# A decode layer's tile framework replaced by a hand-written dependency tracker

## The chip, the cores and the metric

The kernel runs on one core of a Trainium2 chip. The core has five engines, each with its own instruction queue: PE (TensorE, matmuls), DVE (VectorE), ACT (ScalarE), POOL (GpSimd) and SP (SyncE, here only for issuing transfers). Sixteen DMA engines move data between HBM and the on-chip memory SBUF; matmuls write to PSUM, eight banks per partition. The engines order themselves by semaphores: an instruction can wait until a semaphore has reached a value, and can raise one when it is done. The metric is the device time of one execution in microseconds (us).

## The reference

One token (a vector of 1024) goes through a layer norm, then through attention over the last 4096 positions of a cache and a gated feed-forward block; both results are added to the input. Cut to what matters:

```python
xn = _layernorm(x)                                   # 1 x 1024
q = (xn @ wq)                                        # 32 heads of 128
k = k_cache[:, :, Sk - W:, :]; v = v_cache[...]      # 4 key heads, W = 4096
o = softmax(q k^T * 128 ** -0.5) v                   # 8 query heads share a key head
h = gelu(xn @ w_gate) * (xn @ w_up)                  # 3584 wide
out = x + o @ wo + h @ w_down
```

All data is float32. The weights and the part of the cache that is read come to 94.4 MB, each byte is read once, and there is one token to use it for.

## The kernel before

Everything large passes through one SBUF buffer, `ring` (128 partitions x 32768 floats, 16.8 MB). The table `PLAN` (lines 42 to 50) is the order of the work: each entry names a block (`q`, `k`, `v`, `g`, `u`, `o`, `d` for the query, key, value, gate, up, output and down weights or caches), its place in the ring, and the older block whose last use frees that place. The main loop (lines 513 to 561) runs over `PLAN`, does the block's work and calls `used(key)` (line 135), which issues the transfers of every block that waited for this place. So SP's queue holds 24 transfers in `PLAN`'s order, of 0.25 to 8 MB each (lines 117, 120 and 132), and each waits at the head of SP's queue until the readers of the ring place that it overwrites are done.

The projections use both PE and DVE: in `project` (line 251) even rows of the weights go to PE as matmuls (`blocks`), odd ones to DVE as multiply-adds into `part` (`add_scaled`, line 236). `contract` (line 486) does the same for the output and down weights into `out_p` and `out_part`; from row 16 of the down weights on, every row goes to PE. The down weights' last block `("d", 3)` is cut into four rows and the last row into two halves, so that the last transfer is small (lines 111 and 129). At the end `contract` adds the input to the first half of the columns (`y`, line 498), stores it, does the second half (`last_p`, then `y_last`, line 502), and stores that. Each `store` (line 471) issues one transfer from SP (line 474) and one from ACT (line 475).

All of this is written for the tile layer, a framework that allocates buffers from pools, watches which instruction reads and writes which tile, and adds the semaphores. With `manual_schedule` (line 72) it keeps the program's order on each engine. It works as follows here:

- Line 572 builds the program object. Its constructor writes a few constants on POOL and then has all five engines meet in a barrier, with the names of line 572 in the trace.
- Line 581 opens the tile context. The kernel's instructions then stand in a block of their own, and every engine branches into it after the opening barrier.
- Transfers share eight semaphores in turn ("lanes"). A transfer that takes a lane again waits on its own queue until the lane's last transfer has landed.
- With the four engines that count (PE, DVE, ACT, POOL) that makes 12 semaphores. An instruction that must wait for more than its own wait field holds gets separate wait instructions ahead of it on its queue.
- When the context closes, all engines branch to an end block, with line 581's name. There SP waits for the last transfer of all eight lanes and for the counts of DVE, ACT and POOL; five wait instructions hold two semaphores each, and a drain the last. Then comes a barrier of all engines led by POOL; POOL resets the DMA state of the 12 semaphores (a drain), clears them with one range instruction (EVENT_SEMAPHORE_RANGE_CLEAR), and a second barrier of all engines follows.

Of the kernel before, what the change touches and what calls it, by code (L numbers as in the profile page):

```python
# [2 lines left out]

# [5 lines left out]

F32 = mybir.dt.float32  # L10
AF = mybir.ActivationFunctionType
ALU = mybir.AluOpType
AX = mybir.AxisListType
PSUM = bass.MemoryType.PSUM

P = 128
D = 1024
# [7 lines left out]
NB = 512  # L25
# [10 lines left out]
GELU_C = math.sqrt(2.0 / math.pi)  # L36

ROW = (31, 32, 95, 96)


RING = 32768
# [8 lines left out]
]  # L50


@with_exitstack
def tile_decode_layer(
    ctx: ExitStack,
    tc: tile.TileContext,
    x: bass.AP,
    k_cache: bass.AP,
    v_cache: bass.AP,
    wq: bass.AP,  # L60
    wo: bass.AP,
    w_gate: bass.AP,
    w_up: bass.AP,
    w_down: bass.AP,
    out: bass.AP,
):
# [42 lines left out]
    def load(key, at):  # L109

        parts = {("d", 2): 2, ("d", 3): 4}.get(key, 1)
        first = at
        if key[0] in "kv":

            dst = ring[:, at:at + RING // 4]
            if key[0] == "v":
                nc.sync.dma_start(dst, sources(*key)[0])
            else:
                for odd in range(2):
                    nc.sync.dma_start(dst[odd:P:2], sources(*key)[0][:, odd])  # L120
            loaded[key] = ring[:, at:at + RING // 4]
            return
        for src in sources(*key):
            rows, n = src.shape[1:]
            dst = ring[:, at:at + rows * n].rearrange("p (t n) -> p t n", n=n)
            at += rows * n
            step = rows // parts
            for t in range(0, rows, step):
                cuts = 2 if key == ("d", 3) and t == rows - 1 else 1
                for cut in range(cuts):  # L130
                    cols = slice(cut * n // cuts, (cut + 1) * n // cuts)
                    nc.sync.dma_start(dst[:, t:t + step, cols], src[:, t:t + step, cols])  # L132
# [108 lines left out]
    acc, part = {}, {}  # L241
# [182 lines left out]
    rows = (P, 32 * (NA - 4))  # L424
# [43 lines left out]
    y = work.tile([P, CO], F32, name="y")  # L468
    y_last = work.tile([P, CO // 2], F32, name="y_last")

    def store(h, rows):

        dst = out.rearrange("a b (h c n) -> h (a b c) n", h=2, c=4)[h]
        nc.sync.dma_start(dst[0:2], rows[ROW[0]:ROW[0] + 2, :])
        nc.scalar.dma_start(dst[2:4], rows[ROW[2]:ROW[2] + 2, :])

    def accumulate(p, z, t, w, start, stop):
        w = w.rearrange("p (h c n) -> p c h n", c=4, n=CO // 2)
        z = z.rearrange("p t m -> p (t m)")
        for c in range(4):  # L480
            at = 32 * (t + c) + 31 - ROW[c]
            nc.tensor.matmul(  # L482
# [30 lines left out]
    for key, _, _ in PLAN:  # L513
        kind, i = key
        if kind == "q":
            project("q", i, loaded.pop(key), range(NR), 8)
        elif kind == "k":
            kn = loaded.pop(key)
            if i == 0:
                projected("q", 8)  # L520
                q_sb = query_rows()
            transpose_keys(2 * i, kn[:, :half], range(8), (1, 4, 6))
            if i == 0:
                queries(q_sb)

            s = scores(2 * i)
            transpose_keys(2 * i + 1, kn[:, half:], range(4), ())
            exponentials(2 * i, s)
            transpose_keys(2 * i + 1, kn[:, half:], range(4, 8), (4, 5, 7))
            s = scores(2 * i + 1)  # L530
        elif kind == "v":
            vn = loaded.pop(key)
            pT = transpose_probs(2 * i)
            exponentials(2 * i + 1, s)
            values(2 * i, pT, vn[:, :half])
            values(2 * i + 1, transpose_probs(2 * i + 1), vn[:, half:])
            if i == 1:
                maxima()
        elif kind == "g":
            project("g", i, loaded.pop(key), range(NR), NA)  # L540
            if i == 1:
                state = factors()
                projected("g", NA)
                gelu()
        elif kind in ("ua", "ub", "u"):
            taken = {"ua": (0, 1), "ub": (2, 3), "u": range(NR)}[kind]
            project("u", i, loaded.pop(key), taken, NA)
            if kind == "ua":
# [12 lines left out]
        used(key)  # L561


_INS = ["A_x", "A_k_cache", "A_v_cache", "A_wq", "A_wo", "B_w_gate", "B_w_up", "B_w_down"]
# [20 lines left out]
```

## Time and profile before

| | |
|---|---|
| time, median of 3 runs | 228.21 us |
| lowest and highest run | 228.16 and 228.23 us |
| span of the profiled execution, first to last instruction | 226.2 us |
| time outside the span, median minus span | 2.0 us |
| HBM read | 94.38 MB |
| PE busy, DVE busy, ACT busy, POOL busy | 52%, 47%, 12%, 0% of the span |

The profile page gives the profiled execution no other time of its own than this span, so 2.0 us is the difference between the timed runs and the span of another execution. A row of a group has the line of the kernel, the engine, the operation, what it writes and reads, the count and the durations. An engine's name with a q (SPq, POOLq) stands for its queue: instructions that wait, branch or issue a transfer and are not counted as busy. A row of the timeline or of the chain of waits begins with its start and its length in us. A row of the windows has, for a stretch of time, each engine's busy time, the granted TensorE clock, the busy share of the 16 DMA engines and what they moved in GB/s.

### The profile page before, as it was taken

The numbers are of one execution on the slowest core, as the hardware profiler recorded it, in microseconds if no ns is written. First come the engines' busy times: TensorE is split into PE (matmuls) and PEld (weight loads), VectorE is DVE, ScalarE is ACT, GpSimd is POOL, SyncE is SP. The second block draws the span as 40 slices with busy tenths as digits, with TensorE's granted clock in tenths as the row PEclk, the third lists the DMA queues.
The fourth block names the chain that finished last, engine by engine and source line by source line (L and its number), as shares of the span: only waits on it lengthen the run. The fifth ranks groups of instructions, "written<-read, shape, count | busy, mean of one in ns | idle before, by whom it ended". The sixth has DMA issues, their size and how long they took to land.

```text
span 226.2 us, 2531 instructions
## 1 busy us (share of the span) xinstructions
PE 117.3 (52%) x1107; PEld 59.3 (26%) x1107; DVE 107.2 (47%) x129; ACT 28.0 (12%) x54; POOL 0.7 (0%) x6
## 2 busy tenths in 40 slices
PE   0120900558798861998845390245209906461755
PEld 0010200113654722754611010010004902220322
DVE  7030920591235091336069489249209705993701
ACT  2020000002435400454400310000000000000000
POOL 1000000000000000000000000000000000000000
PEclk9999995587999998599979978559956955855879
DMA  9889899899999899998999999999999999999992
GB/s 371 371 383 545 371 394 533 365 394 443 446 477 456 374 400 440 445 481 385 429 415 421 431 492 416 416 456 452 443 417 429 440 414 388 440 423 406 426 399 88
DMA packets 3242, 94.53 MB, mean 418 GB/s; under 512 B 398, under 2 KB 414, under 8 KB 1056
## 3 DMA queue, kind: packets, MB, share of 16 engines
q1 hardware_dynamic: 3208, 94.38, 97.3%
q8 instruction: 8, 0.13, 0.2%
q10 hardware_dynamic: 24, 0.01, 0.0%
q14 instruction: 2, 0.02, 0.0%
HBM read 94.38 MB, written 0.00 MB: 417 GB/s over the span
## 4 chain that ended last, share of the span: by engine, by line
DMA 80%; DVE 14%; PE 5%; issue 0%; SPq 0%; DVEq 0%
DMA ring<-in_B_w_gate 26%; DMA ring<-in_A_wq 18%; DMA ring<-in_A_wo 14%; DVE part L236 13%; DMA ring<-in_B_w_up 11%; DMA ring<-in_B_w_down 11%; PE out_p L482 5%; DVE part L234 1%; SPq L132 0%; DVE y L498 0%; DVE y_last L502 0%; DVEq L502 0%; DVEq L236 0%
## 5 line engine op out<-in xcount | busy, mean ns | idle before, releaser
L236 DVE SCALAR_TENSOR_TENSOR part<-ring,xz,part 128x3584 f32<-128x3584 f32 (+1 forms) x9 | 37.2, 4130 | 20.8 <-DMA ring<-in_A_wq 12.4
L301 PE MATMUL kt_p<-ident,ring 128*128 128x128 f32 x128 | 20.7, 312 | 8.9 <-DMA ring<-in_A_k_cache 5.9
L246 PE MATMUL acc_q<-ring,xz 128*32 128x512 f32 x64 | 11.8, 909 | 22.6 <-DMA ring<-in_A_wq 22.6
L236 DVE SCALAR_TENSOR_TENSOR out_part<-ring,oz,out_part 128x1024 f32<-128x1024 f32 x15 | 19.3, 1285 | 8.0 <-DMA ring<-in_A_wo 7.5
L482 PE MATMUL out_p<-ring,hz 128*32 128x256 f32 (+1 forms) x160 | 14.1, 519 | 13.6 <-DMA ring<-in_B_w_down 13.6
L482 PE MATMUL out_p<-ring,oz 128*32 128x256 f32 x128 | 12.0, 556 | 17.3 <-DMA ring<-in_A_wo 17.3
L301 PEld LDWEIGHTS kt_p<-ident,ring 128*128 128x128 f32 x128 | 15.6, 157 | 17.0 <-issue 9.9
L303 DVE COPY kT<-kt_p 128x512 f32<-128x512 f32 x12 | 8.1, 690 | 20.3 <-PE kt_p L301 20.3
L246 PE MATMUL acc_u<-ring,xz 128*32 128x512 f32 x56 | 10.5, 823 | 10.9 <-DMA ring<-in_B_w_up 7.1
L305 ACT ACTIVATE kT<-kt_p 128x512 f32<-128x512 f32 x20 | 11.4, 596 | 26.8 <-PE kt_p L301 26.8
L234 DVE TENSOR_SCALAR part<-ring,xz 128x3584 f32<-128x3584 f32 (+1 forms) x3 | 6.5, 2173 | 13.1 <-DMA ring<-in_A_wq 7.3
L236 DVE SCALAR_TENSOR_TENSOR out_part<-ring,hz,out_part 128x1024 f32<-128x1024 f32 x8 | 10.3, 1285 | 3.9 <-DMA ring<-in_B_w_down 3.6
L482 PEld LDWEIGHTS out_p<-ring,hz 128*32 128x32 f32 x160 | 6.3, 146 | 21.5 <-DMA ring<-in_B_w_down 12.1
L482 PEld LDWEIGHTS out_p<-ring,oz 128*32 128x32 f32 x128 | 5.4, 158 | 24.0 <-DMA ring<-in_A_wo 18.3
L246 PE MATMUL acc_g<-ring,xz 128*32 128x512 f32 x56 | 8.9, 712 | 3.8 <-DMA ring<-in_B_w_gate 3.8
L246 PEld LDWEIGHTS acc_q<-ring,xz 128*32 128x32 f32 x64 | 2.8, 160 | 30.8 <-issue 16.3
L354 PE MATMUL o_p<-ring,pT 128*32 128x128 f32 x256 | 8.0, 274 | 1.1 <-ACT pT L343 1.1
L317 DVE TENSOR_REDUCE m<-s_p 128x2 f32<-128x1024 f32 x4 | 4.9, 1225 | 6.2 <-PE s_p L312 6.2
L312 PE MATMUL s_p<-kT,qz 128*32 128x512 f32 x64 | 7.7, 598 | 0.0
L354 PEld LDWEIGHTS o_p<-ring,pT 128*32 128x32 f32 x256 | 6.8, 110 | 2.3 <-ACT pT L343 2.1
L246 PEld LDWEIGHTS acc_u<-ring,xz 128*32 128x32 f32 x56 | 2.1, 137 | 17.7 <-DMA ring<-in_B_w_up 7.9
L199 PE MATMUL xt_p<-ident,x_rows 2*128 2x2 f32 x4 | 0.6, 252 | 10.7 <-DMA x_rows<-in_A_x 10.7
(106 smaller groups left out, 85.6 us busy)
## 6 DMA issues: line engine op xcount, KB each, us to landing
ring<-in_B_w_gate SPq DMA_DIRECT2D x2, 7168.0 KB, 28.4
ring<-in_A_k_cache SPq DMA_DIRECT2D x4, 2048.0 KB
ring<-in_A_v_cache SPq DMA_DIRECT2D x2, 4096.0 KB
ring<-in_B_w_down SPq DMA_DIRECT2D x2, 4096.0 KB
ring<-in_B_w_up SPq DMA_DIRECT2D x2, 3584.0 KB
ring<-in_B_w_up SPq DMA_DIRECT2D x1, 7168.0 KB
ring<-in_B_w_down SPq DMA_DIRECT2D x2, 2048.0 KB
ring<-in_B_w_down SPq DMA_DIRECT2D x3, 512.0 KB, 26.0
```

What stands on the lines that cost most here:

```text
L199: nc.tensor.transpose(xt_p[:, r * NJ:(r + 1) * NJ], x_rows[:, r:NR * P:NR], ident[:NJ, :NJ])
L234: nc.vector.tensor_scalar(total, w, factor, None, op0=ALU.mult)
L236: nc.vector.scalar_tensor_tensor(total, w, factor, total, op0=ALU.mult, op1=ALU.add)
L246: nc.tensor.matmul(acc[kind][32 * c:32 * c + 32, b, :], z, w[:, n * NB:(n + 1) * NB], start=start, stop=stop,)
L301: nc.tensor.transpose(t_p[:, jj * P:(jj + 1) * P], kn[:, j * DH:(j + 1) * DH], ident)
L303: nc.vector.tensor_copy(keys[g][:, i, :], t_p)
L305: nc.scalar.activation(keys[g][:, i, :], t_p, AF.Copy)
L312: nc.tensor.matmul(s_p[32 * c:32 * c + 32, b, :], qz[:, g // 2, :], kT[:, i, :], start=True, stop=True)
L317: nc.vector.reduce_max(m2, s, axis=AX.X)
L354: nc.tensor.matmul(o_p[32 * c:32 * c + 32, g, :], pT[:, b, jj, 32 * c:32 * c + 32], vn[:, j * DH:(j + 1) * DH], start=(b == 0 and jj == 0) ...
L482: nc.tensor.matmul(p[32 * c:32 * c + 32], z[:, at:at + 32], w[:, c], start=start, stop=stop)
```

## The change

The tile layer goes. A class `Flow` stands between the kernel and the engines and builds the program twice: the first pass records what each instruction reads and writes (bit masks of partitions and columns; whole PSUM banks) and which earlier ones it must follow; `planned` strikes out every wait that another wait already implies; the second pass puts in the rest. Each transfer has a semaphore of its own, and so has each engine that is waited for: 32 transfers (24 into the ring, 4 small loads of the input, 4 stores) and four engines, 36 semaphores. Before a transfer no lane has to come free. An instruction with several waits gets separate wait instructions on its queue, as before, with the latest in its own field.

Buffers come from a small class `Pool` that hands out one fixed buffer per tag and turn. The order of the instructions on each engine, the transfers, their sizes and the plan of the ring are the same; the identity matrix is written by the same two POOL instructions without the library's helper.

The kernel's instructions now follow the opening barrier without a branch. At the end `finish` has only POOL wait, for the four stores, one instruction for each, and then reset and clear the 36 semaphores. There is no barrier at the end; the other engines stop after their last instruction.

```diff
+class Flow:
...
+    def issue(self, engine, make):
+        k = len(self.ops)
+        waits, inc = self.plan[k] if self.plan else ((), None)
+        for key, value in waits[:-1]:
+            engine.wait_ge(self.sem(key), value)
+        made = make()
+        if waits:
+            key, value = waits[-1]
+            made.wait_op(self.sem(key), value, "sem-ge")
+        if inc is not None:
+            made.then_inc(self.sem(inc), 16 if inc[0] == "d" else 1)
+        self.note(k, made.ins)
+        return made
+
+    def note(self, k, ins):
...
+                source, from_dma = self.ops[other][:2]
+                if (wrote or writes) and not (
+                    source == engine and not from_dma and not dma
+                    and (engine == ENG.PE or not wrote)
+                ):
+                    needs.add(other)
...
+    def planned(self):
...
+            for key, d in sorted(latest.items(), key=lambda x: -x[1]):
+                if mine.get(key, -1) >= d:
+                    continue
+                asked.append((key, d))
+                for other, tick in after[d].items():
+                    mine[other] = max(mine.get(other, -1), tick)
+                mine[key] = max(mine.get(key, -1), d)
...
+    def finish(self, stores):
+
+        pool = self.nc.gpsimd
+        if self.plan:
+            for k in stores:
+                pool.wait_ge(self.sem(("d", k)), 16)
+        numbers = [s.num for s in self.sems.values()]
+        if numbers:
+            span = range(min(numbers), max(numbers) + 1)
+            assert len(span) == len(numbers)
+            pool.dma_reset(span)
+            pool.sem_clear(span)
...
+class Queue:
+    def __init__(self, flow, engine):
+        self.flow, self.engine = flow, engine
+
+    def __getattr__(self, name):
+        call = getattr(self.engine, name)
+        return lambda *a, **k: self.flow.issue(self.engine, lambda: call(*a, **k))
...
-    nc = tc.nc
-    consts = ctx.enter_context(tc.tile_pool(name="consts", bufs=1))
-    stream = ctx.enter_context(tc.tile_pool(name="stream", bufs=1))
-    work = ctx.enter_context(tc.tile_pool(name="work", bufs=1))
-    psum = ctx.enter_context(tc.tile_pool(name="psum", bufs=1, space=PSUM))
-    ctx.enter_context(tc.manual_schedule())
+def decode_layer(nc, x, k_cache, v_cache, wq, wo, w_gate, w_up, w_down, out):
+    consts = stream = work = Pool(nc.nc, "sbuf")
+    psum = Pool(nc.nc, "psum")
...
-    make_identity(nc, ident)
+    nc.gpsimd.memset(ident, 0.0)
+    nc.gpsimd.affine_select(
+        out=ident, in_=ident, compare_op=ALU.not_equal, fill=1.0, base=0,
+        pattern=[[-1, P]], channel_multiplier=1,
+    )
...
-        nc.sync.dma_start(dst[0:2], rows[ROW[0]:ROW[0] + 2, :])
-        nc.scalar.dma_start(dst[2:4], rows[ROW[2]:ROW[2] + 2, :])
+        for queue, c in ((nc.sync, 0), (nc.scalar, 2)):
+            stores.append(len(nc.ops))
+            queue.dma_start(dst[c:c + 2], rows[ROW[c]:ROW[c] + 2, :])
...
-    with tile.TileContext(nc) as tc:
-        tile_decode_layer(tc, *args, res)
+    for _ in range(2):
+        nc = bacc.Bacc("TRN2", target_bir_lowering=False, num_devices=1)
...
+        flow = Flow(nc, plan)
+        flow.finish(decode_layer(flow, *args, res))
+        plan = flow.planned()
```

More of the change, by code (lines that the diff above doesn't have):

```diff
@@ L1 @@
 import math
-from contextlib import ExitStack
 import concourse.bass as bass
-import concourse.tile as tile
 from concourse import mybir
-from concourse._compat import with_exitstack
-from concourse.masks import make_identity
 F32 = mybir.dt.float32
@@ L38, with bits, __init__, sem @@
 ROW = (31, 32, 95, 96)
+SIZES = {"tp": NB, "acc": 2 * NB, "part": 8 * NB, "rows": 2 * NB}
+def bits(dims):
+    total = 1
+    for step, count in dims:
+        if step:
+            grown = 0
+            for i in range(count):
+                grown |= total << (step * i)
+            total = grown
+    return total
+class Flow:
+    def __init__(self, nc, plan=None):
+        self.nc = nc
+        self.plan = plan
+        self.ops = []
+        self.touched = {}
+        self.sems = {}
+        self.first = None
+        for name in ("tensor", "vector", "scalar", "gpsimd", "sync"):
+            setattr(self, name, Queue(self, getattr(nc, name)))
+    def sem(self, key):
+        if key not in self.sems:
+            self.sems[key] = self.nc.alloc_semaphore("flow_%s_%s" % key)
+        return self.sems[key]
+    @staticmethod
+    def place(access):
+        tensor = access.bass_ap.tensor
+        if tensor.space == bass.MemoryType.DRAM:
+            return None
+        row = math.prod(list(tensor.shape)[1:])
+        (step, count), *rest = [tuple(x) for x in access.ap]
+        first, col = divmod(access.offset, row)
+        parts = bits([(max(step // row, 1), count)]) << first
+        if tensor.space == bass.MemoryType.PSUM:
+            return tensor.name, (1 << 128) - 1, bits_of_banks(bits(rest) << col)
+        return tensor.name, parts, bits(rest) << col
+    def issue(self, engine, make):
[12 more added lines that the diff above has]
+    def note(self, k, ins):
+        dma = isinstance(ins, mybir.InstDMACopy)
+        engine = ins.engine
+        needs = set()
+        for access, writes in [(a, False) for a in ins.ins] + [(a, True) for a in ins.outs]:
+            if not isinstance(access, mybir.PhysicalAccessPattern):
+                continue
+            where = self.place(access)
+            if where is None:
+                continue
+            name, parts, cols = where
+            log = self.touched.setdefault(name, [])
+            kept = []
+            for other, wrote, p, c in log:
+                if other == k or not (p & parts and c & cols):
+                    kept.append((other, wrote, p, c))
+                    continue
+                source, from_dma = self.ops[other][:2]
[4 more added lines that the diff above has]
+                    needs.add(other)
+                covered = writes and not p & ~parts and not c & ~cols
+                if not covered or source == engine and not from_dma and not dma and not wrote:
+                    kept.append((other, wrote, p, c))
+            kept.append((k, writes, parts, cols))
+            self.touched[name] = kept
+        self.ops.append((engine, dma, needs))
+    def planned(self):
+        known = {}
+        after = []
+        waits = []
+        counted = set()
+        for k, (engine, dma, needs) in enumerate(self.ops):
+            mine = known.setdefault(engine, {})
+            asked = []
+            latest = {}
+            for d in needs:
+                key = ("d", d) if self.ops[d][1] else ("e", self.ops[d][0])
+                latest[key] = max(latest.get(key, -1), d)
+            for key, d in sorted(latest.items(), key=lambda x: -x[1]):
+                if mine.get(key, -1) >= d:
+                    continue
+                asked.append((key, d))
+                for other, tick in after[d].items():
+                    mine[other] = max(mine.get(other, -1), tick)
+                mine[key] = max(mine.get(key, -1), d)
+            asked = [
+                (key, d) for n, (key, d) in enumerate(asked)
+                if not any(after[later].get(key, -1) >= d for _, later in asked[:n])
+            ]
+            waits.append(asked[::-1])
+            counted.update(d for _, d in asked)
+            done = dict(mine)
+            done[("d", k) if dma else ("e", engine)] = k
+            after.append(done)
+        ticks, totals = {}, {}
+        for k in sorted(counted):
+            engine, dma, _ = self.ops[k]
+            if not dma:
+                totals[engine] = totals.get(engine, 0) + 1
+                ticks[k] = totals[engine]
+        plan = []
+        for k, (engine, dma, _) in enumerate(self.ops):
+            inc = None
+            if dma:
+                inc = ("d", k)
+            elif k in ticks:
+                inc = ("e", str(engine).split(".")[-1])
+            plan.append((
+                [
+                    (("d", d), 16) if key[0] == "d"
+                    else (("e", str(key[1]).split(".")[-1]), ticks[d])
+                    for key, d in waits[k]
+                ],
+                inc,
+            ))
+        return plan
+    def finish(self, stores):
[9 more added lines that the diff above has]
+            pool.sem_clear(span)
@@ L469, in tile_decode_layer @@
     y_last = work.tile([P, CO // 2], F32, name="y_last")
+    stores = []
     def store(h, rows):
         dst = out.rearrange("a b (h c n) -> h (a b c) n", h=2, c=4)[h]
[L474 to L475 removed]
+        for queue, c in ((nc.sync, 0), (nc.scalar, 2)):
+            stores.append(len(nc.ops))
+            queue.dma_start(dst[c:c + 2], rows[ROW[c]:ROW[c] + 2, :])
     def accumulate(p, z, t, w, start, stop):
@@ L561, in tile_decode_layer @@
         used(key)
+    return stores
 _INS = ["A_x", "A_k_cache", "A_v_cache", "A_wq", "A_wo", "B_w_gate", "B_w_up", "B_w_down"]
```

62 lines of the change are left out of this document (38 added, 24 removed).

## The prediction

> **What bounds the kernel now.** I read the page's top first, then the chain of waits, then the windows of the transfers, and last the queue instructions at both ends of the span.
>
> ```profile
> span 226.2 us, 2531 instructions
> PE 117.3 (52%) x1107; PEld 59.3 (26%) x1107; DVE 107.2 (47%) x129; ACT 28.0 (12%) x54; POOL 0.7 (0%) x6
> DMA  9889899899999899998999999999999999999992
> DMA 80%; DVE 14%; PE 5%; issue 0%; SPq 0%; DVEq 0%
> ```
>
> No engine is busy for much over half of the span, while the row of the 16 DMA engines stands at eight or nine tenths in every slice but the last, and 80% of the chain that ended last are transfers. How full the transfers run is seen better in windows (busy share and GB/s are the last two columns):
>
> ```profile
> 0.00:4.00 4.00, 0.00 (x0) 0.00 (x0) 2.79 (x10) 1.28 (x1) 0.70 (x6) 1.00 0.78 263
> 4.00:56.00 52.00, 18.02 (x96) 5.81 (x96) 19.79 (x29) 2.98 (x5) 0.00 (x0) 0.84 1.00 431
> 56.00:108.00 52.00, 40.95 (x424) 27.27 (x428) 21.00 (x32) 19.02 (x39) 0.00 (x0) 0.93 1.01 436
> 108.00:160.00 52.00, 25.50 (x223) 8.16 (x211) 31.14 (x33) 4.68 (x11) 0.00 (x0) 0.80 1.00 430
> 160.00:212.00 52.00, 24.94 (x264) 14.21 (x264) 30.24 (x26) 0.00 (x0) 0.00 (x0) 0.64 0.99 424
> 224.00:226.20 2.20, 0.00 (x0) 0.00 (x0) 0.09 (x1) 0.00 (x0) 0.00 (x0) 1.00 0.01 2
> ```
>
> From 4 us to 212 us the DMA engines never stand still: 0.99 to 1.01 busy at 424 to 436 GB/s. So there are three stages with three limits: a head until the first transfer is issued, one unbroken stream, and a tail after the last bytes. Semaphores can move the head and the tail. In the stream they matter only if a transfer were issued so late that the DMA engines ran dry.
>
> The tail in the chain of waits and in the timeline:
>
> ```profile
> 194.21 23.85 DMA ring<-in_B_w_down
> 218.09 5.16 PE out_p L482 x64
> 223.28 0.43 DVE y L498
> 223.81 0.29 DVE y_last L502
> ...
> 223.73 0.32 SPq L474 DMA_DIRECT2D out_y<-y  x1
> 223.73 0.26 ACTq L475 DMA_DIRECT2D out_y<-y  x1
> 224.12 0.26 ACTq L475 DMA_DIRECT2D out_y<-y_last  x1
> 224.14 0.25 SPq L474 DMA_DIRECT2D out_y<-y_last  x1
> ```
>
> The arithmetic is over at 223.81 + 0.29 = 224.1 and the last store is issued at 224.14; the span ends at 226.2. What fills those two microseconds are queue instructions of the tile context's closing line. The first rows are those that start from 225.3 to 225.5, the others those from 225.55 on (durations in ns as min/median/max, then first and last start):
>
> ```profile
> L581 SPq EVENT_SEMAPHORE  x1: 28/28/28, 225.4 to 225.4; - x1
> L581 SPq DRAIN  x1: 7/7/7, 225.5 to 225.5; - x1
> ...
> L581 POOLq EVENT_SEMAPHORE  x4: 17/17/17, 225.6 to 226.1; - x4
> L581 SPq DRAIN  x2: 7/7/7, 225.6 to 225.8; - x2
> L581 PEldq EVENT_SEMAPHORE  x2: 51/51/51, 225.7 to 226.2; - x2
> L581 POOLq DRAIN  x2: 34/56/78, 225.8 to 226.0; - x2
> L581 POOLq EVENT_SEMAPHORE_RANGE_CLEAR  x1: 96/96/96, 225.9 to 225.9; - x1
> ```
>
> SP's last wait for a lane is through at 225.4, so the last store has landed by then. Everything behind it, 0.8 us, is closing work: SP's two drains, first barrier (225.6 to 225.7), reset and clear (225.8 to 225.9), second barrier (226.0 to 226.2), whose last instruction, on PE, runs 51 ns and ends the span at 226.25.
>
> **The change, part by part.** *Head: the branch goes.* SP's release from the opening barrier and its first transfer:
>
> ```profile
> L572 SPq EVENT_SEMAPHORE  x1: 17/17/17, 0.7 to 0.7; - x1
> ...
> 0.73 0.88 SPq L132 DMA_DIRECT2D ring<-in_A_wq  x2
> ```
>
> The wait was asked for in the window 0.6 to 0.7, so it starts between 0.65 and 0.70 and is over 17 ns later; 0.01 to 0.06 us remain until 0.73, and the branch stands in them. Its cost is therefore between 0 and 0.06; I take the middle, 0.03. The stream begins that much earlier, and since it has no gap all behind it moves too. The opening barrier stays.
>
> *Stream: waits on lanes go, each transfer has its own semaphore.* I cost all of it at nothing. The cover is the queue of transfers already issued:
>
> ```profile
> ring<-in_B_w_gate SPq DMA_DIRECT2D x2, 7168.0 KB, 28.4
> ring<-in_B_w_down SPq DMA_DIRECT2D x3, 512.0 KB, 26.0
> SPq L132 <- DMA ring<-in_A_k_cache: 3.1, 1, 3.1
> ```
>
> A gate block is 7.34 MB, at 431 GB/s 17.0 us of transfer, yet it takes 28.4 us from issue to landing: it stands 11.4 us behind others. A 512 KB piece of the down weights takes 1.2 us and lands after 26.0, so it waits 24.8. Earlier issues, such as the 3.1 us that SP spent waiting on a landing of the key cache, only lengthen that queue. Below 11 us of delay nothing is lost either; beyond that each microsecond costs one. On the compute engines the waits are the same in kind; one fewer or more of 17 to 51 ns (the wait instructions in the rows above) disappears behind transfers in the same way.
>
> *Last rows of the down weights.* PE works from 218.09 to 223.25 without a wait, partly on a backlog at half clock:
>
> ```profile
> 218.09:221.50 3.41, 3.40 (x32) 1.58 (x36) 0.00 (x0) 0.00 (x0) 0.00 (x0) 0.50 0.96 376
> PEld last_p L482 <- PE out_p L482: 0.3, 1, 0.3
> ```
>
> Ahead of `last_p` a separate wait instruction on PE may go, up to 0.05 by the 51 ns above. It would not reach the end: `y_last` also needs `y`, which ends at 223.28 + 0.42 = 223.70, just before 223.81, in both kernels. The SP store of `y_last` no longer waits for its lane; it is 0.02 behind ACT's (224.14 against 224.12), so 0 to 0.02. I take 0 for both. If the half-clock stretch falls otherwise, this stage moves a little: with none, `y` and `last_p` would be ready sooner and at most 0.1 is saved (from 223.81 back to `y`'s end at 223.70); 32 instructions in 3.40 us are 0.85 for a row of eight at half clock against 0.43 at full, so a slow stretch over the last half row would add 0.2.
>
> *End: two barriers, five double waits and two drains go; four waits, a reset and a clear on POOL remain.* POOL starts seven instructions (four waits, two drains, the clear) between 225.6 and 226.1, six steps in 0.5 to 0.55, so 0.09 a step. After the change POOL has stood at the waits since the identity was written, with nothing queued behind but the reset and the clear; nobody waits for it. Its first two waits, for the stores of `y`, are through early. The third, for SP's store of `y_last`, is released when that lands, by 225.43 (SP's wait of 225.4 saw it). Then the fourth wait (+0.09), the reset (+0.09), the clear (+0.09) and its 0.10: 225.80. Against 226.25 this saves 0.45.
>
> The reset and the clear cover 36 semaphores instead of 12, which no row shows. By the rows, a cost that is all for the semaphores would triple: 0.096 to 0.29 for the clear and 0.078 to 0.23 for the drain, together 0.34 more; a cost that is all for the instruction adds nothing. More semaphores cannot make it cheaper. I take 0, because each stays one instruction, and hold 0.34 as the far end.
>
> The Trainium skill, "Runtime: NRT & Kernel Launch", section "The ~15µs preamble/postamble breakdown", gives about 1.5 us for resetting 51 semaphores on an engine, 29 ns each. By that, as an estimate, 24 more would add 0.7 us, and the sum would be 228.4. The row disagrees: 12 in 96 ns are at most 8 ns each.
>
> *Sum.* 226.25 - 0.03 - 0.45 = 225.77 for the span. The median of the runs, 228.21, stands 1.96 above the span; held fixed, that gives **227.73**, 0.21% below the median.
>
> **The rivals.**
>
> 1. *The clear grows with its range.* For it: three times as many semaphores. Against: at 8 ns each the instruction would have no cost of its own. It gives 227.73 + 0.2 to 0.34, so 227.9 to 228.1.
>
> 2. *The time ends with POOL's own last instruction.* If what follows the span begins on each engine alone and then waits for the last engine, the end of POOL counts, not that of PE. POOL's last instruction starts at 226.1 and takes 17 ns, so before 226.16, after 225.80: 0.36 instead of 0.45, and 227.82 with the head. For it: the span's end before is PE's slower reaction to a release that POOL gave. The Trainium skill, same page and section, has after the kernel a barrier that waits for all engines, then a reset; by that rule an engine that is done early gains nothing. The trace ends before it and can't show it.
>
> 3. *The early end of the other engines counts.* SP and ACT would be done at 224.14 + 0.25 = 224.4, not 226.2. If part of the 1.96 us outside the span is work of each engine for itself, it then lies beside POOL's wait. The cap is 225.8 - 224.4 = 1.4; the nearest thing seen is a pair of barriers, 0.4 us (225.6 to 225.7, 225.9 to 226.2), which I take: 227.3. Against: POOL must still do its own part after its clear.
>
> 4. *Slower: a transfer is issued too late.* If the new tracker makes SP's head wait for a reader one block further on, everything queued behind it on SP waits too. A block of 17.0 us against a cover of 11.4 would leave the DMA engines dry for 5.6 us: 233.3 for one such place. It decides from 11 us of delay. Against: the readers are recorded by exact columns of the ring, and planned waits are only removed where another implies them.
>
> 5. *Nothing comes of it*, because the runs' time holds a fixed closing part that hides the kernel's end: 228.2.
>
> **How the numbers follow.** Forecast 0.52, its own range 227.5 to 227.95 from the bounds of the small terms; rival 1 0.10; 2 0.13; 3 0.14; 4 0.06; 5 0.05. A measurement of this kernel can tell about 0.2%, 0.46 us, from no change, which puts the line at 227.75, right beside the forecast. Of the forecast's 0.52 I count 0.38 below that line and 0.14 above. Faster: 0.38 + 0.14 = 0.52. Same: 0.14 + 0.10 + 0.13 + 0.05 = 0.42. Slower: 0.06. The range 227.3 to 228.1 leaves out rivals 4 and 5 and the lower half of 3.
>
> **What would show it.** Head: the first SP transfer at about 0.70. Stream: the windows up to 212 us again near 1.00 and 430 GB/s, and the last piece of the down weights landing as long after the first issue as now. Tail: on POOL four waits, the last two 0.09 apart at 225.4 and 225.5, one drain and one clear, and no barrier. If the clear takes over 0.2 us, rival 1 holds. If the span falls by 0.48 and the time by another amount, 2 or 3 holds, and the difference is outside the span. A window below 0.95 in the stream would be rival 4, and my prediction would be wrong by microseconds.

## The result, and the profile after

The changed kernel takes 227.68 us (median of 14 runs) against 228.22 for the kernel before (14 runs on the same chip). The ratio is 0.9977, with a 95% interval of 0.9969 to 0.9985: 0.2% faster, 0.5 us. Thirteen of the runs lie between 227.48 and 227.94; one slow run of 270.81 (span 269.0), whose cause is not known, is left out of the ratio.

The profiled execution of the changed kernel took 227.77 us, its span is 225.9. The top of its page, and the shares of the engines in its chain of waits:

```profile
span 225.9 us, 2481 instructions
...
DMA 80%; DVE 16%; PE 2%; issue 0%; SPq 0%; DVEq 0%
```

Fifty instructions are gone, and transfers are still 80% of the chain. The windows of the stream (start and end, length, busy time of PE, PEld, DVE, ACT and POOL, granted clock, busy share of the DMA engines, GB/s):

```profile
4.00:56.00 52.00, 18.07 (x96) 5.78 (x96) 19.75 (x29) 3.03 (x5) 0.00 (x0) 0.84 0.99 430
56.00:108.00 52.00, 40.73 (x424) 26.63 (x428) 20.94 (x32) 19.08 (x39) 0.00 (x0) 0.93 1.02 439
108.00:160.00 52.00, 25.99 (x220) 8.24 (x211) 31.75 (x33) 4.59 (x11) 0.00 (x0) 0.77 1.00 432
160.00:212.00 52.00, 24.80 (x267) 13.97 (x264) 29.58 (x26) 0.00 (x0) 0.00 (x0) 0.64 0.98 420
```

Again 0.98 to 1.02 at 420 to 439 GB/s: the stream has no hole, before or after. What is new stands at the two ends. SP's release and its first transfer at the head:

```profile
L762 SPq EVENT_SEMAPHORE  x1: 17/17/17, 0.7 to 0.7; - x1
...
0.73 0.89 SPq L208 DMA_DIRECT2D ring<-in_A_wq  x2
```

The tail in the timeline:

```profile
223.29 0.42 DVE L208 TENSOR_TENSOR y<-out,x_out 128x256 f32<-128x256 f32 x1 [9.62 <-PE out L208]
...
223.75 0.33 SPq L208 DMA_DIRECT2D out_y<-y  x1
223.75 0.27 ACTq L208 DMA_DIRECT2D out_y<-y  x1
223.82 0.29 DVE L208 TENSOR_TENSOR y_last<-y,tp 128x128 f32<-128x128 f32 x1
224.14 0.26 SPq L208 DMA_DIRECT2D out_y<-y_last  x1
224.15 0.26 ACTq L208 DMA_DIRECT2D out_y<-y_last  x1
```

And POOL's closing instructions (durations in ns as min/median/max, then first and last start):

```profile
L183 POOLq EVENT_SEMAPHORE  x2: 17/30/43, 225.3 to 225.5; - x2
L188 POOLq DRAIN  x1: 102/102/102, 225.5 to 225.5; - x1
L189 POOLq EVENT_SEMAPHORE_RANGE_CLEAR  x1: 226/226/226, 225.7 to 225.7; - x1
```

The first transfer is issued at 0.73 as before, and the last one at 224.15, where it was at 224.14 before. Two wait instructions, one drain and one clear are all that follows (the four waits of the source became two instructions, one of them for two stores, and the drain's own wait); no other engine is at work after 224.41. Three dates of each trace's events, and a difference, say where the gain sits (us from the span's start):

| | last load lands | last store lands | span ends | closing (end less landing) |
|---|---|---|---|---|
| before | 223.16 | 225.42 | 226.25 | 0.83 |
| changed | 223.22 | 225.43 | 225.90 | 0.47 |

Between these two executions all of the 0.35 comes from the closing: 0.36 less, and 0.01 back in the landing.

### The profile page after: what moved, and what is told of

Same layout as the page of the kernel before. It is cut to its first block, busy times and chain, and to the rows that moved or that the text cites. A ratio compares the mean times of both kernels' runs of the same rounds, so it can differ in the third digit from the quotient of the medians.

```text
span 225.9 us, 2481 instructions
## 1 busy us (share of the span) xinstructions
PE 117.4 (52%) x1107; PEld 58.4 (26%) x1107; DVE 107.2 (47%) x129; ACT 28.0 (12%) x54; POOL 0.7 (0%) x6
## 4 chain that ended last, share of the span: by engine, by line
DMA 80%; DVE 16%; PE 2%; issue 0%; SPq 0%; DVEq 0%
DMA ring<-in_B_w_gate 26%; DMA ring<-in_A_wq 18%; DVE part L208 14%; DMA ring<-in_A_wo 14%; DMA ring<-in_B_w_up 11%; DMA ring<-in_B_w_down 11%; DVE out_part L208 2%; PE out L208 2%; DVE y L208 0%; SPq L208 0%; DVE y_last L208 0%; DVEq L86 0%; DVE d L208 0%
## 5 line engine op out<-in xcount | busy, mean ns | idle before, releaser
L208 PE MATMUL acc<-ring,xz 128*32 128x512 f32 x176 | 31.7, 825 | 39.2 <-DMA ring<-in_A_wq 22.9
L208 PE MATMUL tp<-ident,ring 128*128 128x128 f32 x128 | 20.6, 311 | 8.8 <-DMA ring<-in_A_k_cache 6.0
L208 PE MATMUL out<-ring,hz 128*32 128x256 f32 (+1 forms) x160 | 13.9, 515 | 13.7 <-DMA ring<-in_B_w_down 13.7
L208 PE MATMUL out<-ring,oz 128*32 128x256 f32 x128 | 11.8, 551 | 17.3 <-DMA ring<-in_A_wo 17.3
L208 PEld LDWEIGHTS tp<-ident,ring 128*128 128x128 f32 x128 | 15.5, 156 | 16.9 <-DMA ring<-in_A_k_cache 6.9
L208 DVE COPY kT<-tp 128x512 f32<-128x512 f32 x12 | 8.1, 690 | 20.0 <-PE tp L208 20.0
L208 ACT ACTIVATE kT<-tp 128x512 f32<-128x512 f32 x20 | 11.4, 596 | 26.9 <-PE tp L208 26.9
L208 PE MATMUL acc<-part,units 128*32 128x512 f32 x44 | 7.2, 745 | 8.6 <-DVE part L208 8.6
L208 PE MATMUL o<-ring,pT 128*32 128x128 f32 x256 | 8.0, 274 | 1.3 <-ACT pT L208 1.0
L208 PE MATMUL s<-kT,qz 128*32 128x512 f32 x64 | 7.7, 598 | 0.0
```

The lines of the kernel that those rows point to most:

```text
L208: return lambda *a, **k: self.flow.issue(self.engine, lambda: call(*a, **k))
```

## The experiments

The theory, A in the expectations: what the change is worth is the closing, the stretch from the last store's landing to POOL's last instruction, and every part of it is paid one to one in the time. Inside it the clear and the reset grow with the number of semaphores, so part of what the barriers gave was lost again. The rivals: the gain lies in the stream or outside the span (the early end of the other engines); the time follows something other than POOL's end; the stores themselves, and not the closing, are what can still be moved. All kernels below are edits of the changed kernel and compute all of the reference; a ratio is against the kernel before, run beside the edit.

**e1, the barriers back.** The new tracker stays; only the end is as before, with 36 semaphores.

```diff
-                pool.wait_ge(self.sem(("d", k)), 16)
+                self.nc.sync.wait_ge(self.sem(("d", k)), 16)
...
+            self.nc.all_engine_barrier()
             pool.dma_reset(span)
             pool.sem_clear(span)
+            self.nc.all_engine_barrier()
```

> The tracker stays; only the end of the tile layer comes back: SP waits for the four stores, all engines meet, POOL resets and clears the 36 semaphores, all engines meet again. Theory A (all of the gain lies behind the landing of the last store): behind that landing the kernel before spends 0.82 us with 12 semaphores; with 36 the clear takes 0.13 longer as it did after the change, so the span is about 226.3 to 226.4 and the time 228.1 to 228.3, no faster than the kernel before. Rival B (part of the gain comes from the stream: no lanes, fewer waits): the time stays clearly between the two kernels, 227.8 to 228.0.

Measured: 228.07 us (11 runs) against 228.15 before, ratio 0.9998 (0.9989 to 1.0007). The profiled span is 226.1, with a closing of 0.93. Queue instructions of its end:

```profile
L183 SPq EVENT_SEMAPHORE  x2: 28/28/28, 225.0 to 225.2; - x2
...
L190 POOLq EVENT_SEMAPHORE_RANGE_CLEAR  x1: 226/226/226, 225.6 to 225.6; - x1
...
L191 POOLq EVENT_SEMAPHORE  x2: 17/17/17, 225.9 to 226.0; - x2
L191 PEldq EVENT_SEMAPHORE  x1: 51/51/51, 226.1 to 226.1; - x1
```

The time is at the low edge of what theory A gave. The span ends with PE's 51 ns again, as before the change. With the barriers the gain is gone, though the tracker and the missing branch are those of the changed kernel; the closing is 0.93 - 0.47 = 0.46 longer than the changed kernel's, and the median 228.07 - 227.68 = 0.39. The interval of e1 against before is 0.2 us to either side: a gain or loss of that size by the tracker ahead of the closing is not excluded, and since e1's closing is 0.10 longer than before (0.93 against 0.83) while its time is no longer, a gain of 0.1 to 0.2 there is likely.

**e2, a wide clear.** 96 more semaphores that nobody uses, so that POOL clears 132.

```diff
+        for n in range(96):
+            self.sem(("x", n))
         numbers = [s.num for s in self.sems.values()]
```

> 96 more semaphores are allocated and never used, so that the last clear covers 132 instead of 36. If the clear costs by the semaphore (96 ns for 12, 226 ns for 36: 5.4 ns each and 31 ns fixed), it takes 0.75 us here and the span is 0.52 longer than after the change, 226.4; if the 226 ns have another cause, the clear stays near 0.23 and nothing moves. The time then says what ends the run: if it follows POOL's last instruction, it rises by the same 0.52 to about 228.2; if it follows the other engines, which stop 1.5 us earlier, it stays at 227.7.

Measured: 228.38 (11 runs), ratio 1.0009 (1.0000 to 1.0018); span 226.65. Its end:

```profile
L190 POOLq DRAIN  x1: 242/242/242, 225.6 to 225.6; - x1
L191 POOLq EVENT_SEMAPHORE_RANGE_CLEAR  x1: 746/746/746, 225.9 to 225.9; - x1
```

The clear grows from 226 to 746 ns and the drain from 102 to 242: 0.66 together. The profiled span grows by 226.65 - 225.90 = 0.75 (0.09 of it because the last store lands at 225.52), the median by 0.70. That is more than the 0.52 expected, which had left out that the drain grows too. Nobody waits for POOL's clear inside the kernel and all other engines are long done, yet its length is paid in full. So the end of POOL counts in full where POOL is the last.

**e3, an early clear.** The semaphores of the 28 loads are cleared when the last store can be issued, while the stores are under way; 8 are left for the end.

```diff
+        done = self.plan[stores[-1]][0][-1]
+        pool.wait_ge(self.sem(done[0]), done[1])
+        pool.sem_clear(span[:self.loads])
         for k in stores:
             pool.wait_ge(self.sem(("d", k)), 16)
         pool.dma_reset(span)
-        pool.sem_clear(span)
+        pool.sem_clear(span[self.loads:])
```

> POOL waits for the vector engine's last result and clears the 28 semaphores of the loads then, while the stores are on their way; behind the last landing only 8 semaphores are left, the reset stays over all 36. By 5.4 ns a semaphore the last clear takes 0.07 instead of 0.23 us: 0.15 off span and time, 225.75 and about 227.53. If the clear's length has another cause, no change from 227.68.

Measured: 227.51 (7 runs), ratio 0.9969 (0.9958 to 0.9981); span 225.74, closing 0.32. Its end:

```profile
L194 POOLq EVENT_SEMAPHORE_RANGE_CLEAR  x1: 185/185/185, 224.1 to 224.1; - x1
...
L197 POOLq DRAIN  x1: 103/103/103, 225.5 to 225.5; - x1
L198 POOLq EVENT_SEMAPHORE_RANGE_CLEAR  x1: 69/69/69, 225.7 to 225.7; - x1
```

The early clear of 185 ns at 224.1 stands beside the stores and costs nothing; the last one is 69 instead of 226 ns. The closing loses 0.15 and the median 0.17.

**e4, one store instead of two on each row group.** The four rows of the output are laid 31 partitions apart, so that one transfer on SP takes all four, and none goes to ACT.

```diff
-ROW = (31, 32, 95, 96)
+ROW = (31, 62, 93, 124)
...
-        for queue, c in ((nc.sync, 0), (nc.scalar, 2)):
-            stores.append(len(nc.ops))
-            queue.dma_start(dst[c:c + 2], rows[ROW[c]:ROW[c] + 2, :])
+        stores.append(len(nc.ops))
+        nc.sync.dma_start(dst, rows[31:125:31, :])
```

> The four rows of the result lie 31 partitions apart (31, 62, 93, 124) instead of in two neighbouring pairs, so each half of the output is one transfer from SP instead of one from SP and one from ACT; the input is added from one load of the same rows. After the change the four stores landed at 224.88, 225.06, 225.25 and 225.43, 0.18 apart, though the packets of a pair were written within 0.03. If landings follow one another at 0.18 whoever issues them, the last one comes 0.18 earlier, two of POOL's waits go (0 to 0.09), and span and time fall by 0.2 to 0.3, to about 227.45. If a landing takes a fixed time from its issue (1.11 to 1.29 seen), it stays as it was for ACT's or SP's: 0 to 0.18 off, and the pairs' spacing was only the difference of the two queues.

Measured: 228.69 (9 runs), ratio 1.0025 (1.0015 to 1.0035); span 226.44. A miss, and slower. The issue of its stores, and below it that of the changed kernel's:

```profile
L208 SPq DMA_DIRECT2D out_y<-y x1: 737/737/737, 223.5 to 223.5; - x1
L208 SPq DMA_DIRECT2D out_y<-y_last x1: 642/642/642, 224.3 to 224.3; - x1
```

```profile
L208 SPq DMA_DIRECT2D out_y<-y x1: 331/331/331, 223.7 to 223.7; - x1
L208 ACTq DMA_DIRECT2D out_y<-y x1: 268/268/268, 223.8 to 223.8; - x1
L208 SPq DMA_DIRECT2D out_y<-y_last x1: 257/257/257, 224.1 to 224.1; - x1
L208 ACTq DMA_DIRECT2D out_y<-y_last x1: 263/263/263, 224.1 to 224.1; - x1
```

`y_last` is done at 223.98, but SP is still issuing the store of `y` until 223.5 + 0.74, and then needs 0.64 for the next: the last landing is at 226.00. In the changed kernel the four stores land at 224.88, 225.06, 225.25 and 225.43, 0.18 apart; that spacing did go, but it cost more at the issue than it gave. On average over the runs 0.24 of the loss against the changed kernel stands outside the span (last section).

**e5, e3 and e4 together,** and the reset left out (`dma_reset`, the drain of 0.10 us):

```diff
-        pool.dma_reset(span)
```

> Three edits to the end of the changed kernel at once: one store for each half of the output (rows 31 partitions apart), the loads' semaphores cleared while the stores are on their way, and no reset of DMA state at the end, since POOL issues no transfers. If the end behind the last landing is a chain whose steps add up, the store saves 0.18, the clear 0.16 (6 instead of 36 semaphores at 5.4 ns), the reset 0.10 to 0.13 and the waits 0 to 0.09: 0.45 to 0.55 off, a time of 227.1 to 227.25. If the time outside the span absorbs such steps, less than half of it shows, 227.45 or more.

Measured: 228.41 (11 runs), ratio 1.0007 (0.9999 to 1.0016); span 226.43. A miss for e4's reason: the last store lands at 226.27. The closing itself fell to 0.16, behind this last clear:

```profile
L197 POOLq EVENT_SEMAPHORE_RANGE_CLEAR  x1: 67/67/67, 226.4 to 226.4; - x1
```

**e6 and e7, the first gate block issued late.** SP's issue of the block is hung behind DVE's copy of a piece of the transposed keys (an early one in e6, a later one in e7), by a spare transfer of 512 bytes that reads that piece; everything queued behind it on SP waits too. This measures the cover that the prediction put at 11.4 us.

```diff
+    def late(kT, i):
+        stores.append(len(nc.ops))
+        nc.sync.dma_start(spare, kT[0:1, i, 0:P])
+        load(("g", 0), 16384)
...
-            if old == key:
+            if old == key and new != ("g", 0):
                 load(new, at)
...
+            if (g, i) == LATE:
+                late(keys[g], i)
```

> On SP's queue a spare transfer of 512 bytes, out of the transposed keys into an unused tile, stands ahead of the first gate block and makes it wait for the second copy of the transposed keys, which ended at 56.3: the block is issued at about 56.8 instead of 51.2, 5.7 us later. Theory A (the stream is covered by the transfers in front, 11.4 us by my prediction): nothing moves, 227.7 to 227.8. Rival B (waits on SP's queue cost time): up to 5.7 us more.

> The same with the last copy of the second head's transposed keys, which ended at 70.7: the gate block is issued at about 71.2, 20 us late. Theory A: beyond the cover each microsecond costs one. 20 minus 11.4 is 8.6; counted from the landing of the value block in front (61.35) and a first packet 1 us behind the issue, the transfers stand still for up to 11: 236.3 to 238.7. A gap of that length shows in the windows from 60 to 72 us. Rival B: 20 us, 247 or more. Were the compute engines and not the transfers the limit from there on, it would be less than 8.

The block's transfer in the chain of waits, in the changed kernel, in e6 and in e7 (start, length to the landing):

```profile
51.16 28.70 DMA ring<-in_B_w_gate
```

```profile
57.28 22.38 DMA ring<-in_B_w_gate
```

```profile
71.25 21.43 DMA ring<-in_B_w_gate
```

e6 issues it 6.1 us later, and it lands at 79.66 against 79.87 (28.70 after 51.16): covered in full. e6 took 227.93 (12 runs), ratio 0.9986 (0.9976 to 0.9996), 0.25 above the changed kernel's median; the interval overlaps the changed kernel's. In the profiled pair 0.2 of it comes up after this block: the second gate block is issued 0.2 earlier (85.78 against 85.99) and lands 0.2 later (116.42 against 116.23), and the last load is still 0.2 later (223.44). Whether the delay of the first block caused that is not shown.

e7 issues it 20.1 us later. It took 240.68 (4 runs), ratio 1.0569 (1.0531 to 1.0606), more than expected. Its windows around the hole:

```profile
56.00:60.00 4.00, 3.33 (x24) 2.55 (x24) 1.32 (x3) 1.72 (x5) 0.00 (x0) 1.00 0.99 426
60.00:72.00 12.00, 10.70 (x83) 6.55 (x84) 4.51 (x11) 4.74 (x10) 0.00 (x0) 1.00 0.01 3
...
76.00:128.00 52.00, 30.20 (x337) 18.07 (x335) 14.25 (x20) 11.79 (x24) 0.00 (x0) 0.77 0.99 425
```

A share of 0.01 at 3 GB/s is the dry queue that the prediction's slower rival meant. The block lands 92.68 - 79.87 = 12.8 later, and the span is 238.78 - 225.90 = 12.9 longer. So what the block loses at its landing is lost by the span one to one. Of 20.1 us of delay 7.3 were covered, not 11.4: with nothing ahead of it the block still takes 21.4 us from issue to landing, not 17.0. The packets in e7's trace say where the 4.4 us go. The block's first packet starts at 72.46, 1.2 after the issue; 14 of the 16 DMA engines are through with their part by 90.52, the slowest only at 92.18; and it counts as landed at 92.68. What was issued behind it takes nothing from it: the first packet of the next key block starts at 90.03, when an engine has done its part of the gate block. In the changed kernel the block's first packet starts at 60.42, 9.3 after its issue, so it stands 8.1 behind others; the other 0.8 is that e7 needs 20.2 from the first packet to the landing, the changed kernel 19.5.

**e8, a lean end.** e3 without the reset, and the four waits in another order, such that in the built program, where four waits become two instructions and waits of the instruction behind them, the clear itself waits for the store that lands last.

```diff
-        for k in stores:
+        for k in stores[:1:-1] + stores[:2]:
             pool.wait_ge(self.sem(("d", k)), 16)
-        pool.dma_reset(span)
```

> The changed kernel's four stores with a leaner end: the loads' 28 semaphores are cleared once the vector engine's last result is there, the reset of DMA state goes, and POOL's waits are put in an order in which the store that lands last (ACT's half of the last result) is waited for by the last clear itself. Behind that landing (225.43 in the changed kernel's profile) only the clear of 8 semaphores is left, 69 ns by the earlier run, so the span would end at 225.43 + 0.02 + 0.07 = 225.52, 0.37 less than after the change. If the steps of the end add up and the time follows POOL's last instruction one to one, the time is 227.3, 0.37 below the changed kernel's on the same chip. If only clears count and waits and resets are hidden, it equals the run with the early clear, 227.5.

Measured: 227.19 (5 runs), against 228.24 before and 227.61 for the changed kernel on the same chip; ratio 0.9957 (0.9944 to 0.9969). It beats both. Its end:

```profile
L194 POOLq EVENT_SEMAPHORE_RANGE_CLEAR  x1: 183/183/183, 223.8 to 223.8; - x1
...
L196 POOLq EVENT_SEMAPHORE  x2: 17/120/224, 224.7 to 224.7; - x2
L197 POOLq EVENT_SEMAPHORE_RANGE_CLEAR  x1: 68/68/68, 225.1 to 225.1; - x1
```

The second wait holds POOL until about 224.9, and the clear starts at 225.1 by itself, when the last store has landed (225.10); the span ends at 225.19: the closing is down to 0.09, little more than the clear of 8 semaphores. From 0.47 that is 0.38 less, and the median fell by 0.42 against the changed kernel's on the same chip.

**e9, two stores of two rows each, 31 partitions apart,** to see whether it was the four rows or their distance that made e4's issue long.

```diff
-ROW = (31, 32, 95, 96)
+ROW = (31, 62, 93, 124)
...
-            queue.dma_start(dst[c:c + 2], rows[ROW[c]:ROW[c] + 2, :])
+            queue.dma_start(dst[c:c + 2], rows[ROW[c]:ROW[c] + 32:31, :])
```

> Four stores as after the change, but the two rows of each are 31 partitions apart instead of neighbours (rows 31, 62 and 93, 124). It asks why one store of four rows at that distance took 640 to 740 ns on SP's queue against 257 to 331 for a pair. If the distance makes the issue long, a pair takes clearly over 330 ns here and the time is 0.1 to 0.4 above the changed kernel's; if the number of rows does, a pair takes 257 to 331 as before and the time is 227.7.

Measured: 228.76 (8 runs), ratio 1.0024 (1.0014 to 1.0034); span 226.83, last landing at 226.30. The issues:

```profile
L208 SPq DMA_DIRECT2D out_y<-y x1: 727/727/727, 223.5 to 223.5; - x1
L208 ACTq DMA_DIRECT2D out_y<-y x1: 652/652/652, 223.5 to 223.5; - x1
...
L208 ACTq DMA_DIRECT2D out_y<-y_last x1: 609/609/609, 224.2 to 224.2; - x1
L208 SPq DMA_DIRECT2D out_y<-y_last x1: 716/716/716, 224.3 to 224.3; - x1
```

Two rows far apart take 609 to 727 ns to issue, as four did (642 and 737); two neighbours take 257 to 331. It is the distance, not the number of rows; distances of 1 and 31 alone were compared. The cost was underestimated: the time is 1.15 above the changed kernel's on the same chip (e10 below), not 0.1 to 0.4. Both issues on SP are long and the second waits for the first, so SP's last one ends 0.75 later than in e10 (225.03 against 224.29), and the last store lands 0.99 later (226.30 against 225.31).

**e10, the changed kernel again,** beside e8 and e9.

> The changed kernel itself on the same chip as the lean end, so that the two compare directly: 227.6 to 227.75, a ratio of 0.9977 to the kernel before.

Measured: 227.61 (10 runs), ratio 0.9975 (0.9965 to 0.9984): the result stands on a second set of runs. Its closing is again 0.47, but its last rows of the down weights fell at full clock. Here is the stretch of 3.41 us near the end that ran at half clock in the profiled changed kernel, first there, then in e10 with its `y_last`:

```profile
218.04:221.45 3.41, 3.27 (x32) 1.55 (x36) 0.00 (x0) 0.00 (x0) 0.00 (x0) 0.50 0.95 371
```

```profile
218.04:221.45 3.41, 3.00 (x48) 1.35 (x48) 0.00 (x0) 0.00 (x0) 0.00 (x0) 1.00 0.99 389
```

```profile
223.71 0.29 DVE L208 TENSOR_TENSOR y_last<-y,tp 128x128 f32<-128x128 f32 x1 [0.20 <-PE tp L208]
```

PE does 48 matmuls at clock 1.00 where it did 32 at 0.50. Without the backlog `y_last` waits 0.20 for PE's last rows, and so for the last load, and no longer for `y`: it ends 0.83 after the last load has landed, where the kernels with the half-clock stretch need 0.89 to 1.01.

## Why the prediction was right, step by step

**Head, 0.03 for the branch: 0.** The first transfer is issued at 0.73 in both kernels; of the 0 to 0.06 that the row left, the low end holds.

**Stream, nothing, under a cover of 11.4 us: nothing, but the cover was mis-sized.** The last load lands at 223.22 against 223.16, and the windows are as full. That earlier issues gain nothing shows too: without the wait for a lane the last piece of the down weights is issued at 197.3 instead of 198.5, and lands no earlier. The slower rival's point of decision is 7.3 us by e7, not 11; the step that failed is the subtraction of the pure transfer time, 17.0, where e7 shows 21.4 for a block with nothing ahead: bytes over bandwidth leave out the 1.2 ahead of the first packet, the slowest of the 16 DMA engines and the landing. The change does not come near either (the first gate block is issued at 51.16 against 51.24 before), and e7 shows that the rival's mechanism is real.

**Last rows of the down weights, nothing, with 0.1 saved or 0.2 added by the clock: held.** The two executions compared both have the half-clock stretch. Where it is missing (e1, e4, e8, e10), `y_last` ends 0.06 to 0.2 sooner after the last load. That belongs to the single execution and not to the change, since the changed kernel itself shows both (its profile here and e10); it may be part of why its runs spread over 0.46 us.

**End, 0.45 less: 0.36 in the profiled pair.** This is the term that was mis-sized. The clear took 226 ns instead of 96 and the drain 102 instead of 78, 0.15 more, where the prediction took nothing and held 0.34 as the far end. On the other side the four waits came as two instructions, so one step fewer stands behind the last landing, which gives back about 0.06. The prediction's own test, a clear of over 0.2 us, speaks for rival 1, and its mechanism is shown: clears of 8, 12, 28, 36 and 132 semaphores took 68, 96, 184, 226 and 746 ns, some 29 ns and 5.4 for each. So neither end of the bracket held: three times the semaphores cost 2.35 times as much. The Trainium skill ("Runtime: NRT & Kernel Launch", "The ~15µs preamble/postamble breakdown") has 1.5 us for 51 semaphores of the runtime's own reset; the prediction's estimate from it, 29 ns for each, is five times what the kernel's clear needs, and the measurement decides. Rival 1's time of 227.9 to 228.1 did not come, because the clear and the drain added 0.15 and not 0.2 to 0.34, and because of the next term.

**Outside the span, 1.96 held fixed: 1.83 to 1.85.** The 1.96 set the median of the runs against the span of one execution that was faster than most. The later runs list both for each: before, spans of 226.36 on average (27 runs beside e1) and 1.83 outside; changed, 225.82 (13 runs) and 1.85. So two errors lean against each other in 227.73: the closing came out 0.10 longer than forecast (0.47 against 225.80 - 225.43 = 0.37), and the constant was 0.1 too large. That the forecast lies within 0.05 of the measured 227.68 is luck in part. On averages the span fell by 0.53 and the time by 0.51, 0.36 of it the closing. The rest of the span, 0.17, would be an earlier landing of the last store, which the prediction had at 0.03. The other kernels with the tracker and these stores have it too, by mean span less closing: 225.38 for e1 with its barriers, 225.42, 225.33 and 225.27 for e2 (closing 1.13), e3 and e8, against 225.53 before; e6 alone, with its late block and a closing of 0.49, has not (225.59). But closings are known from one execution each, or two for the changed kernel. So a saving of 0.1 to 0.25 ahead of the closing is likely, and what makes it stays open.

**The rivals.** 2 (the time ends with POOL's last instruction): e2 shows that POOL's end counts in full, but by that rival the time outside the span should have grown by 0.09, from PE's 51 ns end to POOL's; it grew by about 0.02, and is 1.81 in e1 (PE ends last) against 1.85 (POOL ends last), while the kernel before itself varies from 1.83 to 1.87 between sets of runs. At most half of the rival is there, and none of it is shown. 3 (the early end of the other engines counts): not seen; it is 1.85 although SP and ACT end 1.5 us earlier than POOL, and was 1.83 when all ended together. 4: no window below 0.98. 5: excluded by e1, e3 and e8, whose times follow the closing.

**All of it together.** Four kernels with the same stores, by closing and median: e1 0.93 and 228.07, changed 0.47 and 227.68, e3 0.32 and 227.51, e8 0.09 and 227.19. The closing explains 0.84 of 0.88 us. The kernel before, with 0.83 and 228.15 beside e1, is not on this line: it is no faster than e1 although its closing is shorter, which is the open 0.1 to 0.25 again.

## What to carry to other kernels

When a stream of transfers fills the whole span, look for the worth of a change of dependency tracking behind the last store's landing first (here 0.36 of 0.53 us): list the instructions between that landing and the end one by one, and move ahead of the landing what need not wait for it. Price a bookkeeping instruction by its size, not by its count, and clear early whatever is no longer needed. To turn a span into a forecast of the time, take the span and the time of the same execution, not one execution's span and the runs' median.

## What the runs showed of the hardware

- A store whose two rows lie 31 partitions apart takes 609 to 727 ns to issue, one of two neighbouring rows 257 to 331 (e9, changed kernel); an engine's queue issues the next only after it (e4: `y_last` is done at 223.98, and its store is issued at 224.30, when that of `y`, 0.74 long from 223.51, is out).
- Two small stores that SP and ACT issue at the same time land 0.18 us apart, and the next pair 0.19 to 0.28 behind them (changed kernel, e3, e8). The 0.18 is not a difference between the two queues: of the stores of `y`, ACT's lands first in the changed kernel and SP's in e2. With rows 31 partitions apart the landings stand 0.35 to 0.37 apart (e9).
- A block of 7.34 MB with nothing ahead of it takes 21.4 us from issue to landing, where 431 GB/s would be 17.0 (e7): 1.2 to the first packet, 18.1 until 14 of the 16 DMA engines are through, 1.7 more for the slowest, 0.5 to the landing.
- The time outside the span is on average 1.81 to 1.87 us in all kernels but two: in e4 and e5, where SP alone stores and ACT does not, it is 2.09. The distance of the rows is not the reason (e9: 1.85). The reason stays open; in these two alone the trace has a packet of instructions (8 KB) that starts 1.9 us after the span's end.
